# A blocked real FFT with a complex mix and an MoE behind it: the second transform stage issued for two units at a time

## The chip, the cores and the metric

One NeuronCore of one Trainium2 chip runs the whole kernel as one launch. The metric is the time of the execution on the device in microseconds (us), the median of the runs; less is better.

## What is computed

The reference, cut to what matters:

```python
# x: (8, 3072, 256); w_r, w_i: (256, 256)
X = np.fft.rfft(x, axis=1)
Yr = Xr @ w_r - Xi @ w_i + b_r
Yi = Xr @ w_i + Xi @ w_r + b_i
Y = softshrink(Yr, 0.01) + 1j * softshrink(Yi, 0.01)
y = np.fft.irfft(Y, n=3072, axis=1)
# the rows of y as tokens: w_in (256, 2048), w_out (2048, 256), both float64
h = y.reshape(-1, 256) @ w_in
g = np.where(h >= 1, h, np.where(h <= -1, 0, (h + 1) ** 2 / 4))
return g @ w_out
```

## The kernel before, in words

A sequence of 3072 is taken as 48 x 64, and the transform is done in two steps each way. Fast matmuls in a rounded format are made exact enough by splitting each operand in a high and a low part and adding three products: high by high, high by the weights' low part, and low by high. ScalarE rounds to the high part, VectorE subtracts to get the low part.

**Stage 1** (`stage1`, line 173) transforms along the 48, one "half" of two columns at a time, 128 halves for the eight sequences. Its result is copied by ScalarE (line 179) and stored to DRAM as `z_d` (line 183).

**Stage 2** (`stage2`, line 193) works on a *unit*: two of the 24 frequency groups of one sequence, so 12 units a sequence and 96 in all. It reads the unit's `zin` (loaded by `load_z`, line 188, three buffers) and the unit's part of the table `t_sb`, and does four plain float32 matmuls, which the trace shows as eight records on line 199. The result goes to a PSUM bank of the tag "D", of which there are three.

**`split_X`** (line 209) rounds that result on ScalarE to `Xh` (line 215), and VectorE subtracts to `Xl` (line 216). **`planes`** (line 219) adds the negated imaginary planes on ScalarE (line 224). **`mix`** (line 233) is the product with `w_r` and `w_i`, 24 matmuls a unit (line 246), into a bank of tag "C". **`shrink`** (line 251) adds the bias and does the soft threshold on VectorE (lines 259, 264, 266). **`split_Y`** (line 269) makes `yh` on ScalarE (line 273) and `yl` on VectorE (line 274). **`stage3`** (line 277) is the first step back: six matmuls (line 283) into a bank of tag "D", which ScalarE copies to `ust` (line 287) and SyncE's queue stores (line 291).

The kernel writes the order of every engine out by hand (`manual_schedule`, line 561). Each engine's instructions stand in the order of the calls, in the loop at lines 617 to 669. There is one pass for each `u` from 0 to 98. Pass `u` does, in this order: ask for the `zin` of unit `u + 2`; store finished stage-1 halves and the `ust` of unit `u - 3`; **stage 2 and split of unit `u`**; the low parts `xl` of the stage-1 halves of this pass (one or two, four for every three passes, until pass 79); `split_Y` of unit `u - 2`; the planes of unit `u`; `mix` of unit `u - 1`; stage 1 of this pass's halves, with their copies, loads and the next rounding `xh` on ScalarE; `shrink` of unit `u - 1`; `stage3` of unit `u - 2` and its copy.

For TensorE that is: stage 2, mix, stage 1, stage 3. For ScalarE: `Xh`, `yh`, planes, stage-1 copies, `xh`, `ust`. For VectorE: `Xl`, `xl`, `yl`, the bias and threshold.

Between these, in passes 2 to about 65, the MoE weights are taken from their raw float64 bits and split (`weight_steps`, line 370). Each pass does three small steps, one after `split_Y` and two inside `shrink`; one block of weights takes six, so two passes. VectorE does most of it, ScalarE some (lines 322, 345, 367) and GpSimd the rest (lines 336, 346, 347, 368). `w_in` comes first, then `w_out` from about pass 36 on.

The table `t_sb` has four quarters. The first is loaded ahead of the loop (line 567), the second, third and fourth in passes 1, 4 and 7 (lines 638 to 640); unit 3 is the first that reads the second quarter, unit 9 the first that reads the fourth. Every sequence uses the same table, so each quarter is loaded once.

After the loop comes the last step back, then the MoE, which fills the time from about 570 us on. The change does not touch it.

Of the kernel before, what the change touches and what calls it, by code (L numbers as in the profile page):

```python
# [94 lines left out]
def tile_fft_mix_moe(  # L95
# [65 lines left out]
    def split_x_hi(h):  # L161
        a = xin.pop(h)
        hi = first_st.tile([Q, HT, D], F32R, tag="xh", bufs=2, name="xh")
        lo = first_st.tile([Q, HT, D], F32R, tag="xl", bufs=2, name="xl")
        nc.scalar.copy(hi, a)  # L165
        xs[h] = a, hi, lo

    def split_x_lo(h):
        a, hi, lo = xs[h]
        nc.vector.tensor_tensor(out=lo, in0=a, in1=hi.bitcast(F32), op=ALU.subtract)  # L170
        xs[h] = hi, lo

    def stage1(h, tag, copy):
        hi, lo = xs.pop(h)
        zst[h] = first_st.tile([Q, HT, D], F32, tag="zst", bufs=3, name="zst")
        ps = psum.tile([P, HT, D], F32, tag=tag, bufs=1, name="ps_f1")
        for k, (w, mv) in enumerate(((0, hi), (1, hi), (0, lo))):
            nc.tensor.matmul(ps[:Q], lhsT=c1_sb[:, w, :], rhs=mv, start=k == 0, stop=k == 2)  # L178
        copy(zst[h], ps[:Q])

    def store_z(h):
        b, m = divmod(h, 2 * NJ)
        nc.sync.dma_start(z_d[b][:, m * HT : (m + 1) * HT, :], zst.pop(h))
# [4 lines left out]
    def load_z(u):  # L188
        b, v = divmod(u, NU)
        zin[u] = fold.tile([P, 2, D], F32, tag="zin", bufs=3, name="zin")  # L190
        nc.sync.dma_start(zin[u], zg[b][:, 2 * v : 2 * v + 2, :])

    def stage2(u):
        b, v = divmod(u, NU)
        z = zin.pop(u)
        ps = psum.tile([P, 2, ND, 2, R2], F32, tag="D", bufs=3, name="ps_f2")
        for gi in range(2):
            for d in range(ND):
                nc.tensor.matmul(  # L199
                    ps[:, gi, d].rearrange("p c s -> p (c s)"),  # L200
                    lhsT=z[:, gi, d * P : (d + 1) * P],
                    rhs=t_sb[:, 2 * v + gi, :],
                    start=True,
                    stop=True,
                )
        xp[u] = ps


    def split_X(u):
        ps = xp[u]  # L210
        hi = fold.tile([P, 2, ND, 3, R2], F32R, tag="Xh", bufs=2, name="Xh")
        lo = fold.tile([P, 2, ND, 3, R2], F32R, tag="Xl", bufs=2, name="Xl")
        p4 = ps.rearrange("p g d c s -> p (g d) (c s)")
        h4, l4 = (a.rearrange("p g d c s -> p (g d) (c s)") for a in (hi, lo))
        nc.scalar.copy(h4[:, :, R2:], p4)
        nc.vector.tensor_tensor(out=l4[:, :, R2:], in0=p4, in1=h4[:, :, R2:].bitcast(F32), op=ALU.subtract)  # L216
        xp[u] = hi, lo

    def planes(u):
        b, v = divmod(u, NU)  # L220
        hi, lo = xp[u]
        h4, l4 = (a.rearrange("p g d c s -> p (g d) (c s)") for a in (hi, lo))
        for a in (h4, l4):
            nc.scalar.mul(a[:, :, :R2], a[:, :, 2 * R2 :].bitcast(F32), -1.0)
        first = None
        if v == 0:
            first = x0
            for f, a in zip(x0, (hi, lo)):
                nc.gpsimd.tensor_copy(f, a[:, 0, :, 0:2, :].bitcast(F32))
                nc.gpsimd.memset(f[:, :, :, 0:1].bitcast(F32), 0.0)  # L230
        xp[u] = hi, lo, first

    def mix(u):
        hi, lo, first = xp.pop(u)
        ps = yp[u] = psum.tile([P, 2, D], F32, tag="C", bufs=3, name="ps_mix")
        for gi in range(2):
            n = 0
            for d in range(ND):
                for nm in "ri":
                    if nm == "i" and first is not None and gi == 0:  # L240
                        ah, al = (a[:, d].rearrange("p c s -> p (c s)") for a in first)
                    else:
                        o = 1 if nm == "r" else 0
                        ah, al = (a[:, gi, d, o : o + 2, :].rearrange("p c s -> p (c s)") for a in (hi, lo))
                    for a, k in ((ah, "h"), (ah, "l"), (al, "h")):
                        nc.tensor.matmul(  # L246
                            ps[:, gi, :], lhsT=a, rhs=wm[nm, k][:, d, :], start=n == 0, stop=n == 6 * ND - 1
                        )
                        n += 1
# [19 lines left out]
    def split_Y(u):  # L269
        s = yp[u]  # L270
        yh = fold.tile([P, 2, D], F32R, tag="yh", name="yh")
        yl = fold.tile([P, 2, D], F32R, tag="yl", name="yl")
        nc.scalar.copy(yh, s)
        nc.vector.tensor_tensor(out=yl, in0=s, in1=yh.bitcast(F32), op=ALU.subtract)  # L274
        yp[u] = yh, yl
# [13 lines left out]
    def store_u(u):  # L289
        b, v = divmod(u, NU)  # L290
        nc.sync.dma_start(ug[b][:, 2 * v : 2 * v + 2, :], ust.pop(u))
# [90 lines left out]
    def load_u(c):  # L382
        hb, m = divmod(c, JH // JT)
        b, half_b = divmod(hb, 2)
        uin[c] = pools["in"].tile([Q, JT, D], F32, tag="uin", bufs=2, name="uin")
        j = half_b * JH + m * JT
        nc.sync.dma_start(uin[c], u_d[b][:, j : j + JT, :])
# [25 lines left out]
    def prep_sums(i):  # L413
        (b11, b12), (b21, b22) = halves_of(i)
        t = raw_t[i] = pools["in"].tile([P, 4, QT // 2, JH], F32, tag="tsum", name="tsum")
        for to, a, b in ((0, b12, b11), (2, b22, b12), (1, b22, t[:, 0]), (3, b21, t[:, 1])):
            nc.gpsimd.tensor_tensor(out=t[:, to], in0=a, in1=b, op=ALU.subtract)  # L417
# [125 lines left out]
    def halves(u):  # L543

        lo, hi = (min(NH, 2 * NJ + LEAD + 4 * k // 3) for k in (u, u + 1))
        return range(lo, hi)

    def x_ahead(h):
        if h + 5 < NH:
            load_x(h + 5)  # L550
# [4 lines left out]
    def load_t(k):  # L555
        nc.sync.dma_start(t_sb[:, quarter(k), :], t_f[:, quarter(k), :])

    def load_ti(k):
        nc.gpsimd.dma_start(ti_sb[:, :, quarter(k), :], t_i[:, :, quarter(k), :])

    with tc.manual_schedule():
# [43 lines left out]
        def more_weights():  # L605
            next(ws, None)
# [4 lines left out]
        def quarter4():  # L611
            c, d = next(four)
            stage4(c, d)
            stage4_out(c, d)

        U4 = UN - 6
        for u in range(UN + 3):
            hs_u = halves(u)
            if u + 2 < UN:
                load_z(u + 2)  # L620
            while stored < hs_u.start:
                store_z(stored)
                stored += 1
            if 3 <= u:
                store_u(u - 3)
            if u < UN:
                stage2(u)
                split_X(u)
            for h in hs_u:
                split_x_lo(h)  # L630
            if 2 <= u < UN + 2:
                split_Y(u - 2)
                more_weights()
            if u < UN:
                planes(u)
            if u == 0:
                load_ti(0)
            if u % 3 == 1 and u < 9:
                load_t(u // 3 + 1)
                load_ti(u // 3 + 1)  # L640
            if 1 <= u < UN + 1:
                mix(u - 1)
            for h in hs_u:
                stage1(h, "AB"[h % 2], nc.scalar.copy)
                x_ahead(h)
            for h in hs_u:
                if h + 2 < NH:
                    split_x_hi(h + 2)
            if u == 84:
                for _ in ws:  # L650
                    pass
                first_st.release()
                pools["in"] = right("in")
                load_u(0)
                load_u(1)
            if 1 <= u < UN + 1:
                shrink(u - 1, more_weights if 2 <= u < 84 else lambda: None)
            if U4 <= u < U4 + 4:
                quarter4()
                quarter4()  # L660
            if u == U4 + 4:
                prep_sums(0)
            if u == UN:
                quarter4()
            if u == UN + 1:
                quarter4()
                quarter4()
            if 2 <= u < UN + 2:
                stage3(u - 2)
# [120 lines left out]
```

## Time and profile before

| | |
|---|---|
| median of 3 runs | 2754.1 us (2753.4 to 2754.97) |
| the profiled execution | 2748.2 us, its span 2746.1 us |
| TensorE busy | 2715.6 us (99%) |
| VectorE busy | 2083.0 us (76%) |
| ScalarE busy | 2019.8 us (74%) |
| first and last stage-2 matmul | 44.8 and 559.9 us |

The profile is that of one execution; its rows give start and length in microseconds from the start of the span. PE is TensorE's matmuls, PEld its weight loads, DVE VectorE, ACT ScalarE, SPq the queue of SyncE that issues transfers. An `L` number is the line of the kernel. A bracket behind a row is the engine's idle time ahead of it and what ended it. PEclk is the granted share of TensorE's clock, 1.00 for 2.4 GHz and 0.50 for 1.2 GHz. The ends of matmuls are modelled, so busy rows overlap, and starts are what to go by.

### The profile page before, as it was taken

To read this page: it belongs to the slowest core of one execution; us is meant where nothing else is said; L and a number is where in the kernel's file an instruction comes from. 1 tells how busy PE (TensorE), PEld (TensorE's weight loads), DVE (VectorE), ACT (ScalarE), POOL (GpSimd) and SP (SyncE) were. 2 spreads that over 40 slices of the span, in tenths; PEclk is the share of its full clock that TensorE was granted. 3 is DMA by queue.
4 is the path that set the end of the run, shared out by engine and by line. 5 is a ranking of instruction groups with operands and counts; after the bars stand their busy time and mean duration, and the time that the engine had idled before them with its cause. 6 is when DMAs were issued, how large, how long until landed. Compare 5 with 4: busy or idle time off the path is not lost.

```text
span 2746.1 us, 54291 instructions
## 1 busy us (share of the span) xinstructions
PE 2715.6 (99%) x22336; PEld 2671.8 (97%) x22336; DVE 2083.0 (76%) x2934; ACT 2019.8 (74%) x3413; POOL 358.9 (13%) x353
## 2 busy tenths in 40 slices
PE   7999999999999999999999999999999999999998
PEld 5999999999999999999999999999999999999998
DVE  5999887667777777777777777777777777777776
ACT  5777776567777777777777777777777777777776
POOL 0454330010101010101010110101010101010100
PEclk9999999999999999999999999999999999999999
DMA  8766665410000000000000000000101010100000
GB/s 256 249 213 216 214 215 183 133 61 16 21 28 20 28 20 28 21 28 21 28 20 28 21 28 24 24 30 19 34 15 34 15 34 15 34 14 28 9 17 16
DMA packets 121777, 168.50 MB, mean 61 GB/s; under 512 B 10586, under 2 KB 85178, under 8 KB 121530
## 3 DMA queue, kind: packets, MB, share of 16 engines
q1 hardware_dynamic: 120194, 161.69, 18.9%
q8 instruction: 175, 2.87, 0.4%
q0 software_dynamic: 1200, 3.22, 0.4%
q14 instruction: 72, 0.59, 0.1%
q10 hardware_dynamic: 136, 0.13, 0.0%
HBM read 89.50 MB, written 75.50 MB: 60 GB/s over the span
## 4 chain that ended last, share of the span: by engine, by line
PE 96%; DVE 1%; DMA 1%; ACT 1%; issue 0%; SPq 0%; ACTq 0%; DVEq 0%; POOLq 0%
PE accA L518 20%; PE accB L518 20%; PE ps_xv L462 20%; PE ps_yz L462 15%; PE ps_mix L246 9%; PE ps_i L396 4%; PE ps_f L178 3%; PE ps_f L199 3%; PE ps_i L283 2%; DMA xin<-in_x 0%; DMA t_sb<-in_t 0%; DVE xl L170 0%; DVE yl L274 0%; ACT xh L165 0%; DVE Xl L216 0%
## 5 line engine op out<-in xcount | busy, mean ns | idle before, releaser
L470 ACT COPY snap<-ps_xv 128x256 f32<-128x256 f32 x1152 | 423.6, 368 | 519.5 <-PE ps_xv L462 519.5
L504 DVE TENSOR_TENSOR gl<-h,gh 128x1024 fp32r<-128x1024 f32 x385 | 490.5, 1274 | 352.8 <-ACT gh L500 346.9
L495 DVE SCALAR_TENSOR_TENSOR h<-h,r 128x1024 f32<-128x1024 f32 x385 | 488.9, 1270 | 66.3 <-ACT r L491 61.9
L488 ACT ACTIVATE r<-h,half 128x1024 f32<-128x1024 f32 x385 | 442.8, 1150 | 0.0
L462 PE MATMUL ps_xv<-oph,winh 128*128 128x256 f32 x1536 | 437.0, 284 | 1.1 <-ACT snap L470 0.9
L518 PE MATMUL accA<-wouth,gh 128*128 128x256 f32 x1536 | 434.9, 283 | 0.5 <-ACT gh L500 0.5
L518 PE MATMUL accA<-woutl,gh 128*128 128x256 f32 x1536 | 434.4, 283 | 0.0
L518 PE MATMUL accB<-wouth,gh 128*128 128x256 f32 x1536 | 433.0, 282 | 0.0
L462 PE MATMUL ps_xv<-oph,winl 128*128 128x256 f32 x1536 | 432.2, 281 | 0.0
L518 PE MATMUL accB<-wouth,gl 128*128 128x256 f32 x1536 | 432.2, 281 | 0.0
L518 PE MATMUL accB<-woutl,gh 128*128 128x256 f32 x1536 | 432.0, 281 | 0.0
L518 PE MATMUL accA<-wouth,gl 128*128 128x256 f32 x1536 | 430.7, 280 | 1.0 <-DVE gl L504 1.0
L462 PE MATMUL ps_xv<-opl,winh 128*128 128x256 f32 x1536 | 431.5, 281 | 0.0
L491 ACT ACTIVATE r<-r 128x1024 f32<-128x1024 f32 x385 | 410.7, 1067 | 0.1
L500 ACT CAST gh<-h 128x1024 fp32r<-128x1024 f32 x385 | 404.1, 1050 | 2.9 <-DVE h L495 2.9
L417 POOL TENSOR_TENSOR tsum<-yt 128x256 f32<-128x256 f32 x96 | 100.8, 1072 | 1932.7 <-DVE opl L438 1089.6
L481 DVE TENSOR_TENSOR h<-ps_yz,snap 128x512 f32<-128x512 f32 x384 | 262.8, 684 | 83.1 <-PE ps_yz L462 83.1
L462 PE MATMUL ps_yz<-oph,winh 128*128 128x256 f32 x1152 | 323.7, 281 | 0.4 <-ACT oph L434 0.2
L462 PE MATMUL ps_yz<-opl,winh 128*128 128x256 f32 x1152 | 323.2, 281 | 0.9 <-DVE opl L438 0.9
L462 PE MATMUL ps_yz<-oph,winl 128*128 128x256 f32 x1152 | 324.0, 281 | 0.0
L518 PEld LDWEIGHTS accA<-wouth,gl 128*128 128x128 f32 x1536 | 290.7, 189 | 1.6 <-DVE gl L504 1.6
L462 PEld LDWEIGHTS ps_xv<-oph,winh 128*128 128x128 f32 x1536 | 290.1, 189 | 1.7 <-ACT snap L470 1.7
(96 smaller groups left out, 6503.2 us busy)
## 6 DMA issues: line engine op xcount, KB each, us to landing
xin<-in_x SPq DMA_DIRECT2D x128, 192.0 KB
z_d<-zst SPq DMA_DIRECT2D x128, 192.0 KB
zin<-z_d SPq DMA_DIRECT2D x96, 256.0 KB
u_d<-ust SPq DMA_DIRECT2D x96, 256.0 KB
uin<-u_d SPq DMA_DIRECT2D x64, 384.0 KB
out<-ot SPq DMA_DIRECT2D x191, 128.0 KB
wraw<-in_moe_w_in SPq DMA_DIRECT2D x16, 256.0 KB
wraw<-in_moe_w_out SPq DMA_DIRECT2D x16, 256.0 KB
```

Of the source, the lines that this page charges most:

```text
L246: nc.tensor.matmul(ps[:, gi, :], lhsT=a, rhs=wm[nm, k][:, d, :], start=n == 0, stop=n == 6 * ND - 1)
L396: nc.tensor.matmul(ps[:, jj, :], lhsT=a[:, jj, d * P : (d + 1) * P], rhs=c2_sb, start=True, stop=True)
L417: nc.gpsimd.tensor_tensor(out=t[:, to], in0=a, in1=b, op=ALU.subtract)
L462: nc.tensor.matmul(ps, lhsT=win[a][:, p, w, :], rhs=mv[:, m, :], start=start and k == 0, stop=k == 2, skip_group_check=True)
L470: nc.scalar.copy(snaps[n][:, at, :], ups[n][1][:, 0, :])
L481: nc.vector.tensor_tensor(out=hs[n][:, 0:2, :], in0=yz, in1=snaps.pop(n)[:, 0:2, :], op=ALU.add)
L488: nc.scalar.activation(rs[n][:, part], hs[n][:, part], AF.Relu, bias=half, scale=0.5)
L491: nc.scalar.activation(rs[n][:, part], rs[n][:, part], AF.Square)
L495: nc.vector.scalar_tensor_tensor(out=h, in0=h, scalar=1.0, in1=r, op0=ALU.max, op1=ALU.min)
L500: nc.scalar.copy(gs[n][0][:, part], hs[n][:, part])
L504: nc.vector.tensor_tensor(out=gl, in0=hs[n][:, part], in1=gh.bitcast(F32), op=ALU.subtract)
L518: nc.tensor.matmul(o, lhsT=a[:, blk, at : at + P], rhs=wout[w][:, f, :], start=f == 0 and k == 0 and s % 2 == 0, stop=f == NF - 1 and k == ...
```

## The change

In a pass with an even `u`, stage 2 is issued for unit `u` and right behind it for unit `u + 1`; in a pass with an odd `u` no stage 2 is issued. The splitting of each unit's result stays in the unit's own pass, and so does all the rest.

```diff
             if 3 <= u:
                 store_u(u - 3)
+
             if u < UN:
-                stage2(u)
+                if u % 2 == 0:
+                    stage2(u)
+                    stage2(u + 1)
                 split_X(u)
             for h in hs_u:
                 split_x_lo(h)
```

## Rows read from the trace of the kernel before

**Rows 1.** Windows: busy us (instructions) by engine, PEclk, DMA share, GB/s.

```profile
300.00:400.00 100.00, 99.87 (x766) 94.06 (x765) 89.49 (x173) 72.11 (x157) 37.90 (x36) 1.00 0.68 216
```

**Rows 2.** Timeline around the start of pass 47: start, length, engine, line, operation.

```profile
302.87 0.38 SPq L191 DMA_DIRECT2D zin<-z_d  x1
...
304.10 1.05 PE L199 MATMUL ps_f<-t_sb,zin 128*128 128x128 f32 x8
...
304.89 0.57 ACT L287 COPY ust<-ps_i 128x512 f32<-128x512 f32 x1
...
305.11 0.28 PE L246 MATMUL ps_mix<-wm_rl,Xh 128*128 128x256 f32 x1
...
305.22 0.28 PE L246 MATMUL ps_mix<-wm_rh,Xl 128*128 128x256 f32 x1
```

**Rows 3.** Tile zin: what its instructions waited for (us, times).

```profile
  DMA t_sb<-in_t: 1.0, 1
```

**Rows 4.** Timeline of passes 0 to 3, SyncE's queue and TensorE.

```profile
47.84 0.44 SPq L191 DMA_DIRECT2D zin<-z_d  x1
...
50.32 0.42 SPq L556 DMA_DIRECT2D t_sb<-in_t  x1
...
53.60 1.06 PE L199 MATMUL ps_f<-t_sb,zin 128*128 128x128 f32 x8
...
59.35 0.28 PE L283 MATMUL ps_i<-yl,ti_sb 128*128 128x256 f32 x1
...
60.62 1.13 PE L199 MATMUL ps_f<-t_sb,zin 128*128 128x128 f32 x8 [0.99 <-DMA t_sb<-in_t]
```

**Rows 5.** Windows at the end of the kernel, columns as in rows 1.

```profile
2740.00:2742.00 2.00, 0.00 (x0) 0.00 (x0) 0.64 (x1) 0.00 (x0) 0.00 (x0) 1.00 0.41 120
...
2744.00:2746.00 2.00, 0.00 (x0) 0.00 (x0) 0.00 (x0) 0.00 (x0) 0.00 (x0) 0.50 0.06 21
```

**Rows 6.** Timeline of TensorE ahead of the loop and in pass 0.

```profile
43.40 1.17 PE L178 MATMUL ps_f<-xh,c_sb 96*96 96x512 f32 x2 [3.27 <-ACT xh L165]
...
44.79 1.91 PE L199 MATMUL ps_f<-t_sb,zin 128*128 128x128 f32 x8
```

**Rows 7.** Timeline of pass 7, TensorE, then SyncE's queue.

```profile
82.13 1.05 PE L199 MATMUL ps_f<-t_sb,zin 128*128 128x128 f32 x8
...
83.93 0.58 SPq L556 DMA_DIRECT2D t_sb<-in_t  x1
```

**Rows 8.** Timeline of passes 46 and 47: ScalarE, VectorE, TensorE's weight load.

```profile
303.57 0.58 ACT L179 COPY zst<-ps_f 96x512 f32<-96x512 f32 x1 [1.01 <-PE ps_f L178]
...
305.35 0.58 ACT L215 CAST Xh<-ps_f 128x512 fp32r<-128x512 f32 x1
...
305.97 0.69 DVE L216 TENSOR_TENSOR Xl<-ps_f,Xh 128x512 fp32r<-128x512 f32 x1 [0.80 <-ACT Xh L215]
...
308.35 1.22 DVE L274 TENSOR_TENSOR yl<-y,yh 128x512 fp32r<-128x512 f32 x1
...
309.62 0.19 PEld L283 LDWEIGHTS ps_i<-yl,ti_sb 128*128 128x128 f32 x1 [0.18 <-DVE yl L274]
```

**Rows 9.** Timeline of pass 49: VectorE and TensorE.

```profile
318.48 1.24 DVE L274 TENSOR_TENSOR yl<-y,yh 128x512 fp32r<-128x512 f32 x1
...
320.10 0.29 PE L283 MATMUL ps_i<-yl,ti_sb 128*128 128x256 f32 x1
```

**Rows 10.** Waits, 244.1 to 409.3, then 93.2 to 244.1: us, times, longest.

```profile
PEld ps_i L283 <- DVE yl L274: 2.2, 10, 0.2
...
PEld ps_i L283 <- DVE yl L274: 3.0, 3, 1.0
```

**Rows 11.** Timeline of pass 21: VectorE and TensorE.

```profile
163.60 0.68 DVE L274 TENSOR_TENSOR yl<-y,yh 128x512 fp32r<-128x512 f32 x1
...
164.76 0.29 PE L283 MATMUL ps_i<-yl,ti_sb 128*128 128x256 f32 x1
```

**Rows 12.** Line 274 from 409.3 to 484.6: ns min/median/max, first and last start.

```profile
L274 DVE TENSOR_TENSOR yl<-y,yh x14: 679/681/897, 412.4 to 482.4; 128x512 fp32r<-128x512 f32 x14
```

## The prediction

> **What bounds the kernel now.** The change touches the transform loop alone, so I read the windows there: from 300 to 400 us TensorE is busy 99.87 us, VectorE 89.49 and ScalarE 72.11 [rows 1]. Only what makes TensorE wait counts, and VectorE, which feeds it, has little to spare. The timeline gives the price of a second stage: its eight records begin at 304.10, the second mix record at 305.11, and mix records follow each other by 0.11 to 0.12 (305.11 to 305.22), so the block takes 1.01 - 0.12 = 0.89 us, or 0.11 a record, which is the pace of its neighbours. No turnaround shows that a pair could save [rows 2]. One pass of the loop lasts 5.2 us with one half of stage 1 and 5.9 with two.
>
> **Part 1, the transfers that unit u+1 now needs one pass earlier.** Its input was asked for two passes ahead, now one. In 96 units the second stage never waited for its z, only once for the table [rows 3], and the z load issued at 47.84 was there for the matmul at 53.60: at most 5.8 us [rows 4]. A later odd unit, 49, is asked for at 302.87, 1.23 us ahead of pass 47 [rows 2]; it would be needed 0.89 us into pass 48, and pass 47 without its block takes at least 5.2 - 0.89 = 4.3: 6.4 us or more. I cost it at nothing; the cover is that lead. No DMA moves in SP's order, and buffers of z come free earlier or at the same time.
>
> The table of stage 2 is another matter. Its second quarter, first used by unit 3, is issued in pass 1, at 50.32, and the row at 60.62 says that TensorE waited 0.99 us for it, so it landed 10.3 us after issue [rows 4]. Now unit 3 comes right behind unit 2, whose block ends at 53.60 + 0.89 = 54.49. TensorE stands until 60.62, with mix, stage 1 and stage 3 of pass 2 behind it. These took from 54.49 to 59.47 (the last record begins at 59.35, and one spacing later TensorE is free); now they follow the wait: **+5.0 us**. Everything asked for ahead of the table is issued by then, so the landing should stay.
>
> TensorE idles 6.1 us there. At the kernel's end it has no work from 2740 on; the granted clock is still full from 2740 to 2742 and at 0.50, the 1.2 GHz level, from 2744 [rows 5]. How work comes back from that level shows at the start: after 3.27 us of idle time work resumes at 43.40, and the stage-2 block at 44.79 takes 1.91 us [rows 6] where the one at 53.60 takes 1.06 [rows 4]. So work from 43.40 to 46.70, 3.3 us, went at half speed; the same here is worth half of that: **+1.6 us**, and 0 if the clock holds. I take 1.6, since the idle time is longer than what cost the clock at the end. The Trainium skill, page "TensorE: Matmul & The Clock Gate", section "Part 1: The HAM clock gate", holds that idling hands the clock back and that new work has to earn it again; by it the 1.6 is paid, without it the sum below is 2775.9.
>
> The fourth quarter is issued at 83.93, 1.80 us into pass 7 (82.13), and was used in pass 9. Now unit 9 runs in pass 8, which begins 5.2 - 0.89 = 4.3 us after pass 7, at 4.3 + 0.89 = 5.2 us: 3.4 us after issue [rows 7]. Bounds: 10.3 (rows 4) gives 6.9 us of wait, a quick landing none; nearest is the z load with at most 5.8, so at most 2.4. I take the middle, **+1.0**.
>
> **Part 2, the uneven passes.** TensorE's total work stays, but an even pass becomes 0.89 longer ahead of its mix and an odd one 0.89 shorter. Take the pair 46 and 47 [rows 8]. In even pass 46 ScalarE idles 1.01 us until stage 1's copy can start at 303.57. From there it is busy without a gap: the copies end with Xh of unit 47 at 305.35. VectorE idles 0.80 us for that, does Xl at 305.97, then the stage-1 low parts, then yl from 308.35 for 1.22 us, and TensorE's weight load waits 0.18 us for yl until 309.62. In the changed kernel mix of pass 46 and stage 1 behind it come 0.89 later, so this whole chain does, although stage 2 of unit 47 itself is early: Xh of 47 stands behind the copies of pass 46 in ScalarE's queue. The yl matmul of pass 47 would be due at the old time (two blocks, then the same work). So yl is late by 0.89 more: **0.89 us per such pair**. Behind the waiting matmul stand all of TensorE's later passes; VectorE and ScalarE then stand to the next even pass as before. The next pair's own even pass has 0.89 to spare and cannot give it back, since it starts from the delayed TensorE.
>
> Pair 48 and 49 had room: yl ends at 318.48 + 1.24 = 319.72, its matmul starts at 320.10, 0.38 later; 0.05 of it is needed (309.57 to 309.62 above), so 0.89 - 0.33 = 0.56 is lost [rows 9]. From 244 to 409 us, units 36 to 65, the waits show ten units, all odd, of the fifteen odd ones already waiting for yl [rows 10]: 10 x 0.89 + 5 x 0.56 = **+11.7 us**.
>
> From 93 to 244 us three units, all odd, wait [rows 10]: 3 x 0.89 = 2.7. Three (units 9, 21, 33) have 164.76 - 164.28 = 0.48 of room [rows 11]: 3 x 0.46 = 1.4. The others have 0.9 or more, except two whose loss falls where the even unit behind them had waited as much, nought net. Small waits of even units vanish, -0.2. Together **+3.9**. From 409 us no weights are prepared and the median yl takes 0.68 instead of 1.24 [rows 9, 12]: room 0.33 + 0.56 = 0.89, so 0 to 0.2 a unit; I take **+0.2** in all. Units 90 to 93 share the three "D" banks with stage 4 while one is held by the second unit: at most a copy each (0.57, the copy at 304.89, rows 2), taken at 0.
>
> **Sum.** 5.0 + 1.6 + 1.0 + 11.7 + 3.9 + 0.2 = 23.4 us. The profiled execution took 2748.2, which gives 2771.6; the runs shown have a median of 2754.1, 5.9 above it, and against that the forecast is **2777.5 us**.
>
> **Rivals.** (a) *Only the start costs.* If ScalarE's copies were free enough that Xh of the odd unit were not tied to the even pass, the pairs would cost nothing: 7.6 us, 2761.7. For it: VectorE spends less time waiting for Xh in odd passes. Against it: no idle time ahead of Xh at 305.35. Chance 0.12.
> (b) *Worse: a bank.* The second unit's result holds a "D" bank for a pass more, and stage 3 cycles through the other two. Were the bank that stage 2 needs the one whose copy is still to come (304.89 + 0.57 ends 1.36 us into the pass that began at 304.10, rows 2), each of 46 pairs would stand for up to 1.4 us: 2777.5 + 64 = 2841. Against it: stage 2 never waited for that copy, so banks seem to be taken in the order of release. Or every odd unit loses 0.89 and the table's waits reach their upper ends: some 40 us, 2794. Chance of either 0.09.
> (c) *Faster: odd units run ahead.* Their stage 2 is done a pass early; should Xh start 0.89 us or more before its old place, the waits for yl go (2.2 + 3.0 us, rows 10), and the 0.99 for the table if it lands before unit 3 asks, at 54.49 (rows 4): 2754.1 - 6.2 = 2747.9. It decides only if ScalarE reaches Xh early and the table lands within 4.2 us of issue; rows 4 and 8 say neither. Chance 0.04.
> (d) *Nothing measurable:* gain (c) against loss (a), 2754. Chance 0.05.
>
> **How the numbers follow.** The forecast's own case has 0.70. Its range: the low end leaves out the clock and the fourth quarter and halves the pairs (5 + 8 = 13, less the spread of the runs): 2764; the high end adds the upper bound of the fourth quarter and more loss in pairs: 2790. Cases (b) to (d) and part of (a) lie outside, about 0.2. About 0.2% (5.5 us) is what a measurement of this kernel can tell from no change; (a) and (b) are slower than that too: slower 0.91, same 0.05, faster 0.04.
>
> **What would show it.** Right: a row of stage 2 near 60 us with some 6 us of idle time ended by the table; stage-1 records of 1.1 us after it; waits of stage 3 for yl of 0.5 to 1.1 us in every odd pass from 244 to 409 us, some 14 us in sum; passes in pairs of 6.1 and 5.2 us or so; the part behind 575 us unchanged but for the shift. Wrong: no waiting for the table (then 6.6 us of the sum go); yl waits no longer than before (then 15.8 go); stage 2 waiting for ScalarE's copy of stage 3 (then (b)).

## The result, and the profile after

| | before | after |
|---|---|---|
| median of the runs | 2753.75 us (2750.58 to 2754.97) | 2781.41 us (2778.09 to 2783.82) |
| the profiled execution | 2748.2 us | 2778.09 us |
| its span | 2746.1 us | 2776.0 us |

The ratio of after to before is 1.0103, with an interval of 1.0091 to 1.0115: 27.7 us slower. The forecast was 2777.5, in a range of 2764 to 2790. All ratios here are of fast runs; one of the twelve executions of e10_ahead_late, 2902.25 us at a mean granted clock of 0.852, was slow.

The page of the changed kernel gives the span, the busy times and, under heading 4, the chain that ended last.

```profile
span 2776.0 us, 54319 instructions
...
PE 2729.1 (98%) x22336; PEld 2677.8 (96%) x22336; DVE 2080.3 (75%) x2934; ACT 2021.1 (73%) x3413; POOL 362.4 (13%) x353
...
PE 90%; DVE 3%; ACT 3%; DMA 3%; issue 2%; SPq 0%; ACTq 0%; DVEq 0%; POOLq 0%
```

In the kernel before, the chain was:

```profile
PE 96%; DVE 1%; DMA 1%; ACT 1%; issue 0%; SPq 0%; ACTq 0%; DVEq 0%; POOLq 0%
```

The work of no engine has grown by 30 us (TensorE shows 13.5 more, of which part is the same work at a lower clock). What the chain says is where to look: 3% each on VectorE, ScalarE and DMA, where it had 1%. Waits have come in.

**Where they came in.** For this I take, in two traces, the moment at which the last record of stage 3 of the same unit begins, and subtract. This "shift" is constant where both kernels are equally fast and rises where one loses. Stage 3 of unit `u` is done in pass `u + 2`, so the row of unit 33 closes pass 35 and that of unit 63 closes pass 65. Each row is worked out from the two timelines; the last one is the first matmul of the MoE's second layer (line 518).

```
unit    after   e1_table  e2_xh  e4_mid  e7_pair_xh_late  e8_pair_late  e10_ahead_late
1        7.59     5.01     8.70    2.40       2.99            3.46           3.09
11      10.12     8.63     8.61    2.95       3.01            3.64           3.17
33      13.37    11.90     5.13    3.78      -0.48            6.85          -0.43
63      25.56    24.09     2.60    5.80      -3.01           19.14          -3.12
95      26.34    24.87     2.73    5.77      -2.87           19.92          -3.66
MoE     29.89    29.70     6.63   12.22       1.82           20.17          -0.30
```

Up to unit 11 the last three kernels are the kernel before, and still begin 3.0 to 3.5 later, e9_before 1.4: that is the scatter of the start. Much of it is the clock: the stage-2 block of unit 1 takes 1.05 us in before and e9_before, but 1.91 in e8_pair_late and e10_ahead_late, and in e7_pair_xh_late that of unit 3 takes 2.04 where before it took 1.13 [rows 4]. So a column is to be read from row to row, and its first row only within some 3 us. In the changed kernel unit 2's block begins at 53.19, before at 53.60 [rows 4], so there the first row is loss and not scatter.

For the changed kernel: 7.6 us at the start, 5.8 more up to pass 35, 12.2 more up to pass 65, 0.8 to the end of the loop, 3.6 behind it, and nothing in the second layer of the MoE (the spans differ by 29.9).

**The start.** The timeline of passes 0 to 3 answers to [rows 4].

```profile
49.73 0.38 SPq L191 DMA_DIRECT2D zin<-z_d  x1
...
50.83 0.42 SPq L556 DMA_DIRECT2D t_sb<-in_t  x1
...
53.19 1.16 PE L199 MATMUL ps_f<-t_sb,zin 128*128 128x128 f32 x8
...
60.70 2.04 PE L199 MATMUL ps_f<-t_sb,zin 128*128 128x128 f32 x8 [6.35 <-DMA t_sb<-in_t]
...
92.73 0.46 SPq L556 DMA_DIRECT2D t_sb<-in_t  x1
...
95.06 1.05 PE L199 MATMUL ps_f<-t_sb,zin 128*128 128x128 f32 x8
...
96.69 1.16 PE L199 MATMUL ps_f<-t_sb,zin 128*128 128x128 f32 x8 [0.57 <-DMA t_sb<-in_t]
```

The second quarter of the table lands at about the old time (60.70, before 60.62), but unit 3's block now asks for it right behind unit 2's, so the 0.99 us of idle time are 6.35. The block itself takes 2.04 instead of 1.13, which is the clock. The windows of the same kernel show it here and once more at the end of the loop (columns as in [rows 1]):

```profile
50.00:58.00 8.00, 4.35 (x34) 3.79 (x32) 5.81 (x11) 5.14 (x11) 1.06 (x2) 1.00 1.02 326
58.00:60.00 2.00, 0.00 (x0) 0.00 (x0) 0.00 (x0) 0.00 (x0) 0.00 (x0) 0.51 1.21 329
60.00:65.00 5.00, 4.30 (x20) 4.33 (x21) 0.00 (x0) 0.00 (x0) 0.00 (x0) 0.51 0.89 230
65.00:70.00 5.00, 5.00 (x39) 4.60 (x38) 2.03 (x5) 2.56 (x6) 0.00 (x0) 1.00 0.23 66
596.00:600.00 4.00, 2.50 (x21) 2.26 (x20) 1.57 (x3) 2.46 (x6) 0.00 (x0) 1.00 0.91 250
600.00:605.00 5.00, 4.69 (x26) 4.39 (x26) 1.23 (x1) 2.27 (x4) 1.48 (x3) 0.58 0.44 139
605.00:611.00 6.00, 6.00 (x30) 6.00 (x30) 0.29 (x1) 1.76 (x5) 1.35 (x2) 0.50 0.17 36
```

PEclk is 1.00 in the window in which TensorE begins to stand, 0.51 in the rest of that wait and for its first work until about 65 us, then 1.00 again. The last three rows are the 3.6 us behind the loop: full clock until 600, half until 611.

**The uneven passes.** The waits of passes 36 to 65, from 257.3 to 434.8 us, answer to [rows 10].

```profile
DVE Xl L216 <- ACT Xh L215: 22.0, 15, 2.3
...
PEld ps_i L283 <- DVE yl L274: 9.5, 15, 0.7
...
PEld ps_f L178 <- DVE xl L170: 8.5, 20, 0.7
...
PE ps_i L283 <- DVE yl L274: 8.0, 16, 1.6
```

In all fifteen odd passes stage 3 now waits for yl, before it was in ten, and 9.5 us instead of 2.2. Stage 1 waits for its low part xl too, for which the same view of before has no row. Passes 46 and 47, line by line (the idle time in brackets), answer to [rows 8]:

```profile
316.27 1.95 PE L199 MATMUL ps_f<-t_sb,zin 128*128 128x128 f32 x16
...
321.82 0.58 ACT L179 COPY zst<-ps_f 96x512 f32<-96x512 f32 x1 [1.90 <-PE ps_f L178]
...
323.14 0.57 ACT L287 COPY ust<-ps_i 128x512 f32<-128x512 f32 x1
...
323.61 0.58 ACT L215 CAST Xh<-ps_f 128x512 fp32r<-128x512 f32 x1
...
324.23 0.69 DVE L216 TENSOR_TENSOR Xl<-ps_f,Xh 128x512 fp32r<-128x512 f32 x1 [1.08 <-ACT Xh L215]
...
326.61 1.22 DVE L274 TENSOR_TENSOR yl<-y,yh 128x512 fp32r<-128x512 f32 x1
...
327.88 0.19 PEld L283 LDWEIGHTS ps_i<-yl,ti_sb 128*128 128x128 f32 x1 [0.63 <-DVE yl L274]
```

Sixteen records of stage 2 run in a row for 1.95 us: both units are done by 318.2. Yet Xh of unit 47 comes only at 323.61, behind the stage-1 copy, for which ScalarE now idles 1.90 us instead of 1.01 (0.89 more, one block) and behind the ust copy. Everything on VectorE follows: Xl, the xl, yl.

### The profile page after: what moved, and what is told of

The parts are those of the page before. It is cut to its first block, busy times and chain, and to the rows that moved or that the text cites. A ratio compares the mean times of both kernels' runs of the same rounds, so it can differ in the third digit from the quotient of the medians.

```text
span 2776.0 us, 54319 instructions
## 1 busy us (share of the span) xinstructions
PE 2729.1 (98%) x22336; PEld 2677.8 (96%) x22336; DVE 2080.3 (75%) x2934; ACT 2021.1 (73%) x3413; POOL 362.4 (13%) x353
## 4 chain that ended last, share of the span: by engine, by line
PE 90%; DVE 3%; ACT 3%; DMA 3%; issue 2%; SPq 0%; ACTq 0%; DVEq 0%; POOLq 0%
PE accA L518 20%; PE ps_xv L462 20%; PE accB L518 20%; PE ps_yz L462 15%; PE ps_mix L246 6%; PE ps_i L396 4%; PE ps_f L199 3%; PE ps_f L178 2%; PE ps_i L283 2%; DVE xl L170 1%; DVE yl L274 1%; DMA xin<-in_x 1%; ACT xh L165 1%; ACT Xh L215 1%; DMA t_sb<-in_t 0%
```

## The experiments

The theory: two separate losses, the table's second quarter at the start, and in each later pair ScalarE's order, which ties Xh of the odd unit to the even pass's stage 1. Rivals: VectorE is the bound, so that ScalarE's order doesn't matter; or the delay of the start brings the later passes against other transfers, and the pairs themselves cost little.

**e1_table**: the changed kernel, with the table's quarters asked for earlier.

```diff
+            if h == 6:
+                load_t(1)
...
             if u % 3 == 1 and u < 9:
-                load_t(u // 3 + 1)
+                if u < 7:
+                    load_t(u // 3 + 2)
```

> The changed kernel with the table's quarters asked for earlier: the second before the loop, the third in pass 1, the fourth in pass 4. Theory (the table is one of two causes): the wait of 6.35 us near 60 us goes, the clock stays full there, and some 7.5 to 9.5 us of the 27.7 go: 2772 to 2774 us; the waits of odd passes for yl stay. Rival (the transfers of the start are bound by their rate, so the wait only moves): 2779 to 2782, with the waiting elsewhere ahead of 100 us.

Measured: 2778.18 us, ratio to before 1.0091 (1.0076 to 1.0106): a miss for the theory, and 0.8 us short of what the rival had. Its timeline of the same passes:

```profile
50.59 0.38 SPq L191 DMA_DIRECT2D zin<-z_d  x1
...
53.91 1.06 PE L199 MATMUL ps_f<-t_sb,zin 128*128 128x128 f32 x8
...
58.49 1.50 PE L199 MATMUL ps_f<-t_sb,zin 128*128 128x128 f32 x8 [3.53 <-DMA zin<-z_d]
```

The table was there; now unit 3's own z was not. It was asked for at 50.59, in pass 1, and the matmul could start 7.9 us later. So behind the wait for the table stood a second one, as the rival said: 3.53 us where the table's was 6.35, and the start costs 5.0 instead of 7.6. From unit 9 to 11 the shift rises by another 1.5 (7.13 to 8.63): the trace has the clock at half from 117.1 to 120.5 us there.

**e2_xh**: the changed kernel, with the table as it was, and ScalarE's order alone changed: Xh of the odd unit ahead of the even pass's stage-1 copies; Xl stays in the unit's own pass.

```diff
-    def split_X(u):
+    def split_X_hi(u):
...
+    def split_X_lo(u):
...
                     stage2(u + 1)
-                split_X(u)
+                    split_X_hi(u)
+                split_X_lo(u)
...
                 mix(u - 1)
+            if u < UN and u % 2 == 0:
+                split_X_hi(u + 1)
```

> The changed kernel with one thing moved in ScalarE's queue: Xh of the odd unit goes ahead of the stage-1 copies of the even pass, into idle time; its Xl stays where it was. The table is as in the changed kernel. Theory (Xh stands behind the copies of the even pass): waits of stage 3 for yl in odd passes go or fall below 0.3 us, 12 to 17 us less, 2764 to 2769. Rival (VectorE itself is what is late, its bias and threshold starting 0.89 us later behind mix): the waits stay over 0.5 us and the time is 2776 to 2782.

Measured: 2755.63 us, ratio 1.0005 (0.9996 to 1.0014). The direction was the theory's, the size more than it: 8 us below its range. Its waits from 240 to 400 us, which are passes 34 to 63, with the lines from 216 on five further down:

```profile
ACT Xh L215 <- PE ps_mix L251: 20.6, 15, 1.6
...
DVE Xl L221 <- ACT Xh L215: 0.9, 4, 0.2
```

TensorE has no row in this view, neither for yl nor for xl, and VectorE's 22.0 us of waiting for Xh are 0.9. What ScalarE now waits for ahead of the odd unit's Xh is the mix of the even pass: Xh has two buffers, and mix of unit `u - 1` reads the one that Xh of unit `u + 1` is to fill. The start is no better (8.70), but from there to unit 63 the kernel gains 6.1 us on before: it has lost the waits that before itself had [rows 10]. VectorE as the bound falls: by it the waits would have stayed over 0.5 us, and they are gone.

A second thing had changed. The yl step alone, over thirty units each (ns: shortest, median, longest), first before, then e2_xh:

```profile
L274 DVE TENSOR_TENSOR yl<-y,yh x30: 675/950/1243, 247.1 to 407.4; 128x512 fp32r<-128x512 f32 x30
```

```profile
L279 DVE TENSOR_TENSOR yl<-y,yh x30: 676/682/897, 241.1 to 399.0; 128x512 fp32r<-128x512 f32 x30
```

Half of the yl of before took 1.2 us; in e2_xh nearly all take 0.68. In before those of 1.2 us run beside a GpSimd step of the weights, the one at 308.35 [rows 8] beside this:

```profile
307.95 1.06 POOL L347 TENSOR_TENSOR woutl<-val,rest 128x256 fp32r<-128x256 f32 x1
```

In e2_xh yl comes ahead of that step, and the GpSimd step that does run beside it leaves it at 0.68:

```profile
311.67 1.67 POOL L351 TENSOR_TENSOR val<-val,wouth 128x256 f32<-128x256 f32 x1 [6.97 <-ACT wouth L350]
...
311.85 0.68 DVE L279 TENSOR_TENSOR yl<-y,yh 128x512 fp32r<-128x512 f32 x1
...
313.41 1.19 POOL L352 TENSOR_TENSOR woutl<-val,rest 128x256 fp32r<-128x256 f32 x1
...
313.73 0.19 PEld L288 LDWEIGHTS ps_i<-yl,ti_sb 128*128 128x128 f32 x1
```

So an earlier Xh gives twice: the queue, and 0.5 us of yl. The queue alone would do: yl ends at 312.53, 1.20 us ahead of the weight load that needs it, and over the odd ones of units 34 to 63 this lead is 0.57 us at the least. By these figures a yl that took 0.54 longer, as in before, would cost next to nothing (an estimate; no run has the early Xh with the slow yl).

**e4_mid**: e1_table, with the second block behind the even pass's stage 1 instead of ahead of its mix.

```diff
                 if u % 2 == 0:
                     stage2(u)
-                    stage2(u + 1)
                 split_X(u)
...
                 x_ahead(h)
+            if u < UN and u % 2 == 0:
+                stage2(u + 1)
```

> As e1_table, with the second block of stage 2 issued behind stage 1 of the even pass, not ahead of its mix. Theory (the chain begins at the stage-1 copy): that copy is back at its old place, only the copy of stage 3 comes later, by about 0.31 us where ScalarE used to reach it at 304.89; waits for yl fall from 0.5 to 1.1 us to 0.2 to 0.6, some 10 us below e1_table: 2760 to 2765. Rival (any uneven pass costs its 0.89, wherever the block stands in it): as e1_table within 3 us.

Measured: 2758.53 us, ratio 1.0018 (1.0009 to 1.0028), the theory's way and 1.5 us below its range; the rival is out. Stage 1 of the even pass is not pushed back, and from unit 1 to unit 95 only 3.4 us are lost, against 19.9 in e1_table. The wait for yl from 247 to 415 us is 5.1 us in 11 units. Behind the loop the profiled execution, 2760.37, has the clock at half from 580.4 to 594.0 us, and its shift rises by 6.5.

**e5_before_table**: the kernel before with e1's table loads and nothing else.

> The kernel before with the same earlier transfers of the table as e1_table. Theory: only its own wait of 0.99 us goes, 2752 to 2754. Rival (asking earlier slows the first stage, whose transfers are in the way): 1 to 3 us slower, 2755 to 2757.

Measured: 2752.06 us, ratio 0.9998 (0.9988 to 1.0007), as expected. It stood 2.6 us back at unit 2's block (56.16, before 53.60), after a block of unit 1 that took 1.91 us, the length at the lower clock, where before took 1.05, and 1.3 at the end of unit 1, so the wait of 0.99 is regained, which a median can't tell. From unit 1 to unit 95 its shift stays at 1.3 to 1.4: the table loads do nothing further to the loop.

**e8_pair_late**: the changed kernel with its pairs from unit 12 on only.

```diff
-                if u % 2 == 0:
+                if u < 12:
+                    stage2(u)
+                elif u % 2 == 0:
```

> The changed kernel with pairs only from unit 12 on and nothing else. Theory (the start and the odd passes add up): the start's 10 us go, the odd passes' 16 stay: 2768 to 2772. Rival (the pile-up of the start causes the later waits): 2753 to 2760.

Measured: 2773.72 us, ratio 1.0070 (1.0057 to 1.0083), above what was expected by 2 us; the profiled execution took 2768.53. From unit 11 to unit 95 the shift rises by 16.3, in the changed kernel by 16.2. The waits of passes 36 to 65, from 251 to 428 us, have the changed kernel's very rows:

```profile
PEld ps_i L283 <- DVE yl L274: 9.5, 15, 0.7
PEld ps_f L178 <- DVE xl L170: 8.5, 20, 0.7
```

So the later loss does not hang on the start: some 10 us up to unit 11, some 16 behind it. That the delayed start causes the later one is out.

**e7_pair_xh_late**: e8_pair_late with e2's order of ScalarE from unit 12 on.

```diff
+            if 12 <= u < UN and u % 2 == 0:
+                split_X_hi(u + 1)
```

> Pairs only from unit 12 on (units 0 to 11 as in the kernel before), with Xh of the odd unit ahead of the even pass's stage-1 copies as in e2_xh. Theory: the start costs nothing, and from unit 12 on the passes gain what e2_xh gained behind its start, about 6 us: 2746 to 2749, faster than the kernel before. Rival (e2_xh's gain is only the recovery of work that its slow start had piled up): 2752 to 2755, no faster than before.

Measured: 2749.80 us, ratio 0.9986 (0.9978 to 0.9995): less than a us above the expected range, and faster than before. From unit 11 to unit 95 it gains 5.9 us.

**e10_ahead_late**: from unit 12 on no pairs at all; stage 2 of every unit one pass ahead, its Xh ahead of the stage-1 copies.

```diff
-                if u % 2 == 0:
+                if u < 12:
                     stage2(u)
+                    split_X_hi(u)
+                if 11 <= u < UN - 1:
                     stage2(u + 1)
-                split_X(u)
+                split_X_lo(u)
...
+            if 11 <= u < UN - 1:
+                split_X_hi(u + 1)
```

> From unit 12 on stage 2 of each unit is issued one pass ahead, one block in every pass, and its Xh ahead of the stage-1 copies of that pass. Theory: passes are even and Xh is early in each, so the waits for yl of even passes go too: 2744 to 2748, as fast as e7_pair_xh_late or 1 to 2 us faster. Rival (VectorE is the bound in these passes): 2750 to 2754.

Measured: 2748.98 us, ratio 0.9984 (0.9976 to 0.9993). That is a us above the expected range, and a us below the rival's. From unit 11 to unit 95 it gains 6.8 us. It isn't told apart from e7_pair_xh_late; both beat both kernels, the one before by 0.14 and 0.16%, which is less than the 0.2% that the forecast counted as a difference, though the intervals leave 1 out. What helps is Xh early, not the pair.

**e9_before**: the kernel before once more, for its clock.

> The kernel before once more, for the clock where the loop ends (570 to 590 us): the changed kernel and e1 to e5 all fall to half clock there for 7 to 14 us, the profiled execution of the kernel before did not and was 5 us faster than the median of its runs. If that fall is the execution's chance: half clock there in this one, with 2752 to 2756 us, or full clock and 2748 to 2750. If it belongs to the changed kernels alone: full clock and a time over 2752.

Measured: 2749.52 us, with no lower clock behind the loop, as in the profiled execution shown first (2748.2). That is what was expected if the fall comes by chance of the execution. The median of before in the same set is 2753.41. What follows stands in the last section.

## Why the prediction was right, and where its numbers were off

**The bound and the price of a block.** The sum rested on 0.89 us for a block [rows 2] and on no gain from pairing. Right: sixteen records take 1.95 us where eight take 1.05, and ScalarE's idle time ahead of the stage-1 copy rose by just 0.89.

**The table's second quarter, 5.0 + 1.6 = 6.6.** Right in kind, 7.6 in size. The idle time was 6.35 us (6.1 worked out) and the clock did fall, from 58.05 to 64.88 us. Work from 60.70 on went at half of it, 4.2 us, worth 2.1 where the forecast took 1.6; the other 5.5 stand against 5.0. The Trainium skill, page "TensorE: Matmul & The Clock Gate", section "Part 1: The HAM clock gate", holds that idling hands the clock back; by it the clock's term is paid, and the 0.51 in the window of 58 to 60 us agrees.

**"At most 5.8 us", the z loads at nothing.** This step failed, without harm to the sum. The bound was taken from a load of pass 0, and the one that counts, unit 3's, took 7.9 us in e1_table, at a time when the DMA engines are full (a share of 0.99 in its window of 50 to 58 us, 1.02 in the changed kernel's). The table's later wait covered it. Anyone who had repaired only the table on the strength of the forecast would have got 2.6 of the 7.6 us. In later odd passes the cover held: behind the start no stage 2 waits for z.

**The table's fourth quarter, +1.0, bounds 0 to 6.9.** It was 0.57; the quarter landed 4.0 us after its issue (92.73 to 96.69).

**The pairs of passes 36 to 65, +11.7.** It was 12.2, by the shift ten passes at 0.89 and five at 0.65 (forecast 0.56). The path was right: ScalarE's order is shown as the cause by e2_xh, where by the estimate given there the shorter yl is not what removes the waits, and the price of 0.89 by the idle time at 321.82. The waits were divided otherwise than told: those for yl are 9.5 us where some 14 were foretold, and part falls on stage 1 (xl, 8.5 us), since VectorE does xl ahead of yl, a wait that the forecast did not name. It lies ahead of yl in the same pass and is the same delay.

**Passes up to 35, +3.9, and behind pass 65, +0.2.** They came to 5.8 less 0.57 = 5.2, and to 0.8. The three passes priced at 0.89 lost 0.88 or 0.89. The three priced at 0.46, from the room of yl alone [rows 11], lost 0.56 to 0.83: there stage 1 waits for xl, 0.70 us each time, which the forecast left out. Those taken at nothing lost some 0.1 each. This is the largest error of the loop.

**The sum.** In the loop 26.3 us for 23.4. To this come 3.6 behind the loop in the profiled execution, where the forecast had "unchanged but for the shift": the lower clock of 600.8 to 611.0 us. The 5.9 us that led from the profiled execution of before to its median were carried over as they stood. They seem to be this very fall, which that execution lacks (last section), so part of it was in the forecast under another name: the medians are 27.7 us apart, the profiled executions 29.9. That the total came within 4 us of the median is luck to that extent.

**The rivals.** (a), that only the start costs, was refuted by e8_pair_late. (b), the bank: stage 2 waits for no copy in the trace. (c) asked that Xh run ahead, and in the changed kernel it doesn't; but its gain is real once ScalarE's order lets it: 5.9 us in e7_pair_xh_late, where the forecast had 2.2 + 3.0 for the yl waits.

## What to carry to other kernels

Work issued early gained nothing here while the step that takes its result stood where it had stood in another engine's queue: move the consumer too, or move nothing. An even loop made uneven delays all that stands behind the longer part, on every engine that works in order, and the shorter pass didn't give it back. It is not the unevenness itself that costs: with the block behind stage 1 (e4_mid) a sixth of the loss was left, and with Xh moved (e7_pair_xh_late) the same pairs were faster than before. Before a step is moved ahead, look at what it needs just once (a table, a first load), and at what is late next when that is repaired.

## What the runs showed of the hardware

**The clock after short waits.** At the end of the loop TensorE waits for the loads of the last step back. First before, then the changed kernel:

```profile
573.03 2.00 PE L396 MATMUL ps_i<-c_sb,uin 96*128 96x96 f32 x16 [1.26 <-DMA uin<-u_d]
```

```profile
599.62 2.65 PE L396 MATMUL ps_i<-c_sb,uin 96*128 96x96 f32 x16 [1.50 <-DMA uin<-u_d]
```

Nearly the same wait; yet before keeps the full clock there, and the changed kernel has half from 600.8 to 611.0. Over all profiles it fell at this wait in seven (for 6.8 to 13.7 us) and not in before, e8_pair_late and e9_before. Waits of 2.8 us and more at this place all went with a fall; of those of 1.3 to 1.5 us some did, some not. In the loop it was the same: in e1_table the clock is at half from 117.1 us, after a wait for yl of 1.66 us that ended at 116.92, while the same wait of 1.65 us, which ended at 120.00 in the changed kernel, brought no fall. Behind the loop the shift rises by 3.6 us in the changed kernel, 0.2 of it by the longer wait, and by 4.8 in e1_table. The window of e8_pair_late at the same place, for comparison:

```profile
595.00:600.00 5.00, 3.88 (x31) 3.48 (x31) 1.23 (x1) 2.18 (x5) 2.82 (x4) 1.00 0.30 80
```

The profiled execution of e8_pair_late, which kept its clock, took 2768.53, its other runs 2773.42 to 2774.39. The mean granted clock is on record for every execution: 1.000 for that one and 0.996 for the others. So it is with the 48 executions of before in the two later sets: the eight with 0.999 or more took 2749.3 to 2751.3 us, the twenty with 0.997 took 2752.8 to 2756.4, and the twenty with 0.998 lie across both. The scatter of before thus goes with the clock, the 3.9 us between e9_before (0.999) and the median of its set included. Where in an execution the clock was low only the profiled ones show, so that it is this fall in the others is argued, not shown. What decides between a fall and none is open.

**Two engines at one memory.** yl took 0.68 us by itself and 1.22 beside GpSimd's two-operand step in before, as shown under e2_xh. All 27 yl of before that took over 0.8 us have a GpSimd step beside them; but 18 others have one too and aren't slowed. Nor is yl at 311.85 in e2_xh: there VectorE was still at its step before when the GpSimd step began, and it is that one that took 1.67 us. The Trainium skill, page "SBUF — State Buffer", section "SBUF: two separate sides", says that the two engines share a pair of ports which one of them holds for a whole instruction. By that yl at 308.35 would stand until the GpSimd step ends at 309.01 and take 0.66 + 0.68 = 1.34 us, an estimate; the 1.22 measured agrees roughly.
